# Eight more groups of unread products, and a new hand-written order, in a gated delta-rule layer with a softplus MLP

## The chip, the cores and the metric

The kernel runs on one core of one Trainium2 chip. A core has five engines that work side by side, each through a queue of its own: TensorE (PE, matrix products; its weight loads are shown as PEld), VectorE (DVE), ScalarE (ACT), GpSimd (POOL) and SyncE (SP, which here only issues DMAs). The metric is the device time of one execution in microseconds (us); lower is better. A profile is one execution recorded by the hardware profiler.

## The reference, cut to what matters

There are 4 batches of 8 heads, 768 time steps, and 48 features a head. Each head keeps a 48x48 state and runs a gated delta rule; its output, in the layout of 3072 tokens by 384 features, goes through a two-layer network with softplus between.

```python
k_n = k / (np.linalg.norm(k, axis=-1, keepdims=True) + 1e-06)
for t in range(S):
    readout = np.einsum('bhd,bhde->bhe', q[:, :, t], state)
    y[:, :, t] = g[:, :, t] * readout
    v_old = np.einsum('bhde,bhd->bhe', state, kt)
    state = state + bt[:, :, :, None] * np.einsum('bhd,bhe->bhde', kt, vt - v_old)
...
h = x @ w_in                                             # 384 -> 2048
g = np.maximum(h, 0.0) + np.log1p(np.exp(-np.abs(h)))
return (g @ w_out).astype(np.float32)                    # 2048 -> 384
```

## The kernel before

The 768 steps are cut into 12 chunks of 64. Within a chunk the recurrence is rewritten as dense algebra: the Gram matrix of the keys, the inverse of a unit triangular 64x64 matrix for each of the 32 heads, and products with the state that came from the chunk before. Two chunks make a pair; what is said of "inverse 2" is the inverse of the pair of chunks 2 and 3.

The program is built as a list of numbered items. Each has a kind, the engines that may run it, the items that it depends on and the buffers that it uses. Nothing runs in the order in which items are added. A table, `_ORDER`, is read word by word by `emit` (lines 56 to 74). A word such as `D178` says that item 178 is issued now, on VectorE (P is TensorE, D VectorE, A ScalarE, G GpSimd, S SyncE). So the table fixes each engine's own order and, where an item may run on more than one engine, which one does it. It also fixes who gets which buffer: an item's buffer is taken from a ring at the item's first use and goes back after its last use, so an item can have to wait until the last reader of the buffer's former content is done. Which engine is ahead of which is not fixed: that comes out of semaphores on the chip.

The rings that matter: PSUM has five buffers `d` for all products of the scan, two `h` for the first dense layer, and one `o` for the second and for the unread products. Loaded queries (`qf`) have two buffers, loaded keys (`kf`) three, query tiles in half precision (`qn`) two.

The kinds of items, in the order of a pair's work, with their lines:

- `load` (lines 249 and 271): the inputs, by DMAs in SyncE's queue. `wload` (297): quarters of the two weight matrices, `w0` and `w1`, by DMAs in GpSimd's queue.
- `ksq`, `red` (545, 549): squares of the keys on ScalarE, and their sums on VectorE. The root follows: `sqrt` on ScalarE for the first two pairs, `pow` on GpSimd (566) for the others. `eps` (570, 572) adds the small constant and inverts.
- `cast`, `kmul` (327): keys and queries to half precision, the keys times their inverse norm (but for the first pair, which is scaled later). `trs` (345, 388): transposes on TensorE. `kev`: their copy out of PSUM into `kqt`.
- `gram` (503; `gramk`, `gramq`, `gramd` at 461 and 432 for the first pair): products of keys with keys and queries. `kkc` copies the key part to `kk`, `mask` (518, 480) the masked query part.
- `kd0`, `kd1`, `ln` (604, 611): the diagonal blocks are gathered and transposed into a layout in which each partition holds two 16x16 blocks. `clear`, `diag`, `prep` (629) and 15 `step`s (639, 646) then invert those blocks row by row: two small instructions to a step, each dependent on the one before, on VectorE for the first pair and on GpSimd for the other five.
- `cv`, `tn` (667) and `c16`, `t32` (686): two copies of the result, and their transposes. `xmm` (707), `xs`, `tmm` (732), `tlo`, `thi` and `zmm` (770), `z` (779): the blocks are put together to the larger inverse. `xmm` is the first product that reads the inverse.
- The scan of a chunk, for even and odd heads apart: `ks`, `qs` (813; state times keys and queries), `vs` (823; values of the first pair times the norm), `w` (847), `umm` (855), `u1`, `zu` (878), `u2`, `smm` (898) and `s` (913; the new state), `ymm` (928), `y` (943; the output times the gate `g`), `ytr` (962) and `xt` (transposed for the dense part).
- The dense part of a chunk or pair: `g1` (992) in groups of six products, `soft` (1004; softplus on ScalarE), `g2` (1019) in groups of four, `o` (copy) and `store` (1039). Between the roots and the first softplus ScalarE loads another table of functions (`table`, line 1051).
- `warm` (1064): groups of three products of the identity with itself, 512 columns wide, into an `o` buffer. Nothing reads them. `IDLE` (line 98) is the number of groups: 24, in the table as P1232 to P1255. Four groups share one buffer.

Before, the 24 groups stand as follows in TensorE's queue: 15 of them (1232 to 1243, 1248 to 1250) among the transposes and Gram products of the first pair, up to the transposes of q2; two (1251, 1244) right behind the last Gram product of chunk 0; three (1245 to 1247) between the transposes of q3 and `xmm` of chunk 0; and the other four (1255, 1254, 1252, 1253) among the first groups of `g1` and the scan of chunk 1.

Of the kernel before, what the change touches and what calls it, by code (L numbers as in the profile page):

```python
# [74 lines left out]
def kernel(  # L75
# [19 lines left out]
    DM = H * D  # L95
    RAW = (0,)
    ON_ACT = (0, 1)
    IDLE = 24
    FF = moe_w_in.shape[1]
    NF = FF // P  # L100

# [954 lines left out]
    for cs in jobs:  # L1056
        dense(cs)
    for x in range(IDLE // 4):
        wb = Buf(p_o)
# [12 lines left out]


_ORDER = """
S0 D158 P1232 P1234 P1233 P1235 A1 P1236 P1238 D111 P1237 P1239 P114 A9 A104 D105 A110 P112 S8
A106 D115 P1241 D113 P124 P121 A123 D134 P137 A138 D133 P135 P1243 D125 P147 D107 D122 A136 P144
A108 P1240 P127 P1242 A149 P1249 A148 A146 D126 P1248 D109 D156 S19 S18 A145 S2 P1250 A206 P207
S3 A116 A117 A208 P118 A120 S5 S17 A119 P150 A152 S12 A129 S33 A154 D159 S27 S26 D157 D160 D161
D162 D163 D164 D165 D166 D167 D168 D169 D170 D171 P128 S16 D172 D173 D174 P1251 D175 D176 D177
P1244 A197 S25 D198 A222 P223 A224 G179 S11 A140 D178 G238 G239 P1245 A131 P1246 P1247 S24 A199  # L1080
P181 D180 S10 A139 P184 A182 D200 S4 D588 D132 D130 G188 A185 G187 P183 A190 P193 D194 A189 A594
P595 S13 A589 S32 P590 A201 D202 D203 D219 P186 A596 A591 P597 A598 P592 P605 A593 P603 S7 S6
D606 D604 A191 P204 P609 P607 A587 S34 D192 A275 D205 P209 D608 P214 S35 S42 S43 D211 A610 D210
D216 P220 G96 A212 A217 A215 D213 P141 A221 A142 A143 D218 D276 S41 S40 A277 P600 P599 D601 D602
P195 G300 D196 P872 D278 G99 A873 P230 A231 P225 A228 P1255 A226 A233 A235 D232 D229 D227 D611
D234 P874 A875 P886 D236 P619 P612 D620 D613 P151 D155 A284 P884 G98 A887 A885 G97 S14 D237 P285
P1254 A286 P882 P301 A883 A302 P615 A616 S49 P622 A623 P876 S15 A877 P878 G100 G101 G103 P614
P617 G279 D280 P621 P624 D153 S48 A879 A625 A618 G102 D281 P282 D297 P1252 D283 P630 D631 P632
D633 P292 A293 P298 A299 P880 A881 P634 A295 G240 G241 D294 D635 G242 G243 G244 G245 G246 P1253
G247 G248 P303 A304 G249 G250 G251 G252 G253 D306 D307 S50 P308 D296 A309 A311 P904 A905 P916  # L1090
A917 D312 P287 A290 D288 A313 P914 G254 G255 G256 D305 A915 P888 P910 A911 D314 D315 P627 P626
D629 D628 A353 D257 D258 P912 A913 P908 D354 P889 G259 D260 A909 G316 G317 P906 A907 G318 G319
G320 P902 A903 P890 P891 S57 A892 S56 P261 A262 G321 A267 P264 D265 A355 P895 P896 D291 P638
P266 P263 A270 D289 P643 P636 D310 G322 P897 P898 A268 P271 D356 G357 S20 S21 D644 A269 A899
P646 A647 D637 P639 A640 P918 S51 D362 P363 D272 A364 P641 A642 P645 P648 A649 S59 S58 A378 D358
P919 P920 P921 A922 D359 P650 P651 D653 P654 D652 S22 S23 D655 P656 P273 P925 P379 D657 A380
D274 P660 P667 P658 G323 G324 G325 G326 G327 A659 P926 P669 S28 S29 D668 G375 P670 A671 S65 S64
A431 D661 P663 D664 P927 D432 P672 A673 P662 P665 A666 S31 P360 D361 P376 S30 P678 D679 A377
P680 D681 P365 A366 D367 A368 D369 P928 P682 D683 P381 D383 A384 G328 G329 G330 G331 G332 G333
P386 A389 D388 D387 P956 S72 S73 A433 D385 A957 D434 P962 P370 D371 D390 D372 A963 A373 A382  # L1100
P954 A955 P936 A937 A391 P675 S74 P674 P934 G334 A935 G335 D336 S66 D374 S67 G440 G337 D676 S894
S36 D338 D677 D392 P944 S901 A945 S923 P342 A343 D393 P339 P952 A953 S37 S44 A340 A346 P948 A949
P441 P940 A941 A345 P684 P691 D692 D685 A442 P341 P693 P344 D348 G435 D436 A347 D453 P942 A943
S75 P932 A933 P349 P687 P694 S81 S80 P686 G394 S45 D350 A509 G395 G396 G397 G456 G398 P960 G399
S924 S39 A695 A961 A929 P950 D688 P689 D690 P454 S38 A951 P946 A947 P938 S88 A939 P457 G400 A458
G401 G402 G403 G404 G405 D510 P958 A959 S89 P964 G406 G407 S893 S931 S91 P702 D703 S930 S90 P351
S54 P696 D697 D352 A511 D512 P965 P966 P967 D968 S970 G408 G409 G410 P698 A455 P459 A462 D461
D463 P699 D460 D700 P971 P972 D701 P973 P974 P464 D437 S900 P704 A975 S85 S969 P708 A465 P438
D468 A467 D466 D709 D705 P978 P715 D716 P711 A439 A712 P979 P448 D450 D452 D451 D449 P718 S47
S46 S60 G534 G411 S53 G412 A415 A719 D416 P710 P713 A714 P980 P981 P443 D445 D447 P717 P720 A982  # L1110
S52 A444 P726 D727 P985 A721 P706 A446 A469 P728 A424 D729 P722 P723 P535 A536 P730 D707 P986
P987 D731 P1000 S55 G513 A1001 P1014 A1015 D470 S83 D471 A423 P988 A989 P1008 P1010 G413 A1009
D414 P420 A1011 P417 A418 D724 D514 D725 D531 P1018 A1019 P994 A995 A421 P532 D533 D515 P998
A999 P739 P732 D733 S82 A518 P734 P419 P422 D740 G472 G473 G474 G475 D426 P1004 A1005 D425 P996
A997 P429 P427 P742 D430 A743 P735 A736 P1002 D428 A1003 P519 P741 P744 P737 G476 A745 P1020
A1021 D738 S991 S70 D520 G477 S983 P516 P1006 P750 D751 S977 A517 A1007 S69 S976 P542 D544 D545
A543 D546 P752 P992 S71 A993 D753 P1016 A1017 P521 D523 A522 D525 P746 A524 P747 S990 D748 D749
P1022 A1023 P1012 G478 G479 G480 A1013 G481 P526 D530 A527 A529 P537 A540 D539 D538 P763 D541
P1024 P1025 P754 S984 P1026 P1027 D528 P756 P758 S84 A755 S61 D764 P766 S87 A1028 G482 G483 G484
G485 G486 G487 G488 G489 G490 G491 D492 P495 S63 P498 S62 D757 S1030 A767 A499 A496 G547 P759  # L1120
D548 D549 P1031 P1032 P1033 P1034 A1035 S1037 P765 D760 G493 D494 A501 A502 P768 D769 P761 D762
P1038 P1039 P776 D777 P771 P774 P497 P500 S76 A503 P770 D775 P778 D779 P1040 P1041 A1042 P1070
A1071 P1062 A1063 P1045 P1072 A1073 S68 S1036 P1058 A1059 P1046 P1054 A1055 P1074 D772 D773 P780
D781 P787 P1047 A1075 P1048 A1049 P1064 A1065 S77 S1043 P1060 A1061 P783 A784 D788 P790 A791
G550 G551 G552 G553 G554 G555 G556 G557 G558 G559 G560 G561 G562 G563 G564 D504 P505 P1056 S78
A1057 P1080 A1081 P782 D506 P785 D786 G565 G566 G567 G568 G569 G571 P789 P792 D793 P1052 A1053
P1066 A1067 P798 D799 P794 P795 D796 P1078 A1079 D797 P1082 P804 D805 A1083 P813 P811 D812 S79
P507 P807 D572 D508 A580 D570 S1050 S1044 S93 D808 P800 D801 S1029 P814 D815 P1068 A1069 P1076
A1077 P1084 P1085 P1086 P1087 D1088 P816 A817 P806 P809 D810 S95 P576 P573 A574 S1051 P824 D825
P802 A803 S1089 P1091 P1092 P1093 P1094 P818 P822 D823 A577 P578 A1095 S1097 P575 A581 P819 D582  # L1130
D820 P826 A827 S1090 P1098 P1099 P1100 P1101 A1102 S86 S94 S1103 P1132 A1133 P1114 A1115 P1105
P1126 A1127 D821 P828 P837 D829 P835 P583 P1138 A1139 P1116 A1117 P1106 P1107 P1120 A1121 P1108
A1109 S1111 S92 P1140 A1141 D836 D584 D579 P838 A839 P831 A832 P1134 A1135 P1128 A1129 P840 A841
P830 P833 P1112 A1113 S1104 S1110 P848 D834 P846 P843 P842 P1118 A1119 P1130 A1131 D844 D845
P852 P859 P1122 D847 A1123 D849 P850 D851 D860 D853 P1124 A1125 P1142 A1143 P1144 P1136 P1145
P1146 A1137 P1184 A1185 P1147 D1148 S1149 S1150 P1178 P862 D863 P855 D856 P585 D586 A1179 P1158
P1159 P1160 P1161 A1162 P854 P857 A858 P861 P864 P1151 P1152 P1153 P1154 D1155 S1156 S1157 P1172
D865 P1174 P1165 P1166 A1173 A1175 P1167 P1168 D1169 S1170 S1096 P1182 A1183 P1176 A1177 P868
D869 P866 D867 P1186 A1187 P1180 A1181 P870 S1171 P1188 P1189 D871 P1204 A1205 P1208 A1209 P1190
P1191 A1192 S1194 P1206 A1207 S1193 P1212 A1213 P1195 P1196 P1202 P1210 A1203 A1211 P1197 P1198  # L1140
D1199 S1200 S1201 P1216 A1217 P1214 S1163 P1218 P1219 P1220 A1215 P1221 A1222 S1223 S1164 S1224
P1225 P1226 P1227 P1228 A1229 S1231 S1230
"""

# [1 line left out]
_INS = ['q', 'k', 'v', 'beta', 'g', 'moe_w_in', 'moe_w_out']  # L1146
_OUTS = [((3072, 384), 'float32')]


# [23 lines left out]
```

## Time and profile before

| | |
|---|---|
| Median of the runs (lowest, highest) | 255.66 us (254.85, 256.0) |
| The profiled execution's own time | 255.46 us |
| Its span, from the first to the last instruction | 253.6 us |
| PE busy | 236.9 us (93%) |
| DVE, ACT, POOL busy | 153.7, 153.0, 127.1 us |
| Mean granted TensorE clock | 0.966 |
| DMA | 27.56 MB, 109 GB/s in the mean |
| The unread products (line 1064) | 72, 19.3 us busy |
| First dense layer (992), second (1019) | 73.3 and 70.3 us busy, 384 products each |

Busy time counts each engine for itself. The granted clock is the share of its full speed that TensorE was allowed: here 1.00 or 0.50. Matrix products overlap in the array, so that a product's duration is longer than the distance to the next one; what a group costs in a full queue is read from start to start. In a row of the timeline, "x32" counts instructions and the bracket at the end gives the engine's pause before them and what ended it.

### The profile page before, as it was taken

The page shows a single profiled execution, that of the slowest core. Times are in us where ns is not written, and L with a number is a line of the kernel's source. Part 1 is how long each engine was busy: PE and PEld are TensorE (multiplying, and loading weights), DVE is VectorE, ACT ScalarE, POOL GpSimd, SP SyncE. Part 2 cuts the span into 40 slices and gives each one's busy share as a digit, 9 for nine tenths or more (in the row PEclk, how much of TensorE's full clock was granted, in tenths as well). Part 3 has the DMA queues.
Part 4 walks back from the last instruction along what each step waited for, and adds up shares of the span by engine and source line. Part 5 has one row for each costly group of instructions (what it writes and reads, how often), then busy time and mean ns, then how long its engine had stood idle before and what let it go on. Part 6 is the DMA issues. An engine that isn't in the chain of part 4 may idle for free.

```text
span 253.6 us, 11355 instructions
## 1 busy us (share of the span) xinstructions
PE 236.9 (93%) x5040; PEld 160.5 (63%) x5040; DVE 153.7 (61%) x311; ACT 153.0 (60%) x285; POOL 127.1 (50%) x227
## 2 busy tenths in 40 slices
PE   7976588998989999999999999999999999999993
PEld 3543577676766765666766767755676565777751
DVE  7789888775893699759697588523843315313000
ACT  3557777686866579973777675456453475223530
POOL 8201653978879889988948859884000000000000
PEclk9999757799999999999999999999999999999999
DMA  8999999999990789083943850643024130112113
GB/s 111 198 181 178 178 179 180 186 195 176 176 153 6 173 180 157 4 200 83 156 98 84 170 99 22 124 83 80 3 66 93 23 80 0 34 32 48 34 47 78
DMA packets 86192, 27.56 MB, mean 109 GB/s; under 512 B 76288, under 2 KB 86144, under 8 KB 86144
## 3 DMA queue, kind: packets, MB, share of 16 engines
q1 hardware_dynamic: 80096, 23.21, 50.2%
q0 software_dynamic: 3968, 3.25, 8.2%
q10 hardware_dynamic: 2080, 0.39, 1.2%
q8 instruction: 39, 0.64, 1.2%
q14 instruction: 9, 0.07, 0.1%
HBM read 25.26 MB, written 4.72 MB: 118 GB/s over the span
## 4 chain that ended last, share of the span: by engine, by line
PE 76%; DVE 9%; DMA 4%; issue 3%; SPq 2%; ACT 2%; POOL 2%; ACTq 0%; DVEq 0%; POOLq 0%
PE h L992 25%; PE o L1019 23%; PE d L813 4%; DMA beta_l<-in_beta_dram 3%; PE d L855 3%; PE d L732 3%; PE d L770 3%; PE d L878 2%; PE d L928 2%; PE d L503 2%; PE d L707 2%; PE d L898 2%; PE d L388 2%; PE d L345 2%; POOL beta_l L175 2%
## 5 line engine op out<-in xcount | busy, mean ns | idle before, releaser
L1004 ACT ACTIVATE ga<-h 128x512 f16<-128x512 f32 x96 | 56.3, 598 | 33.4 <-PE h L992 27.6
L992 PE MATMUL h<-xt,w_in 128*128 128x512 f16 (+1 forms) x384 | 73.3, 330 | 0.1
L1019 PE MATMUL o<-w_out,ga 128*128 128x384 f16 x384 | 70.3, 326 | 1.4 <-issue 0.7
L1019 PEld LDWEIGHTS <-ga 128*128 128x128 f16 x384 | 35.7, 98 | 23.9 <-issue 1.8
L992 PEld LDWEIGHTS <-w_in 128*128 128x128 f16 x384 | 35.6, 99 | 20.7 <-issue 0.6
L639 POOL TENSOR_TENSOR tmp<-nn,tt 128x30 f32<-128x30 f32 (+7 forms) x75 | 30.1, 401 | 5.6
L646 POOL TENSOR_TENSOR tt<-tt,tmp 128x30 f32<-128x30 f32 (+7 forms) x75 | 29.4, 392 | 5.9
L566 POOL TENSOR_TENSOR nv<-nv,half_c 128x32 f32<-128x32 f32 x4 | 21.8, 5456 | 5.1 <-DVE nv L549 5.1
L218 ACT ACTIVATE kqt<-d 128x1024 f16<-128x1024 f16 (+1 forms) x21 | 18.4, 903 | 7.0 <-PE d L388 6.1
L218 ACT ACTIVATE osb<-o 128x384 f32<-128x384 f32 x18 | 8.8, 489 | 21.5 <-PE o L1019 21.4
L943 DVE TENSOR_TENSOR yg<-d,gf 128x384 f16<-128x384 f32 x24 | 12.8, 553 | 13.6 <-PE d L928 10.2
L1064 PE MATMUL o<-ident 128*128 128x512 f16 x72 | 19.3, 411 | 1.4 <-POOL ident masks.py:199 1.4
L847 DVE TENSOR_TENSOR w<-vf,d 128x384 f16<-128x384 f32 x22 | 11.3, 549 | 12.0 <-PE d L813 10.8
L218 ACT ACTIVATE u<-d 128x384 f16<-128x384 f32 x31 | 14.3, 491 | 7.1 <-PE d L878 3.3
L218 ACT ACTIVATE kk<-d 128x256 f16<-128x256 f32 (+1 forms) x34 | 12.8, 413 | 7.8 <-PE d L503 6.4
L518 DVE TENSOR_TENSOR mt<-d,mask 128x256 f16<-128x256 f32 x40 | 15.5, 418 | 3.2 <-PE d L503 1.9
L220 DVE CAST u<-d 128x384 f16<-128x384 f32 x17 | 9.1, 549 | 13.1 <-PE d L878 11.6
L813 PEld LDWEIGHTS <-kqt 48*64 48x64 f16 x704 | 13.3, 108 | 5.5 <-issue 5.3
L220 DVE COPY osb<-o 128x384 f32<-128x384 f32 x6 | 3.3, 556 | 21.6 <-PE o L1019 21.6
L813 PE MATMUL d<-s,kqt 48*64 48x48 f16 x704 | 16.4, 188 | 0.0
L545 ACT ACTIVATE ksq<-kf 128x768 f32<-128x768 f32 x12 | 10.1, 843 | 7.6 <-DMA kf<-in_k_dram 6.7
L220 POOL CAST tw<-tt 128x256 f16<-128x256 f32 x10 | 5.4, 563 | 16.1 <-DVE tt L646 16.0
(110 smaller groups left out, 380.1 us busy)
## 6 DMA issues: line engine op xcount, KB each, us to landing
qf<-in_q_dram SPq DMA_DIRECT2D x24, 192.0 KB, 5.1
vf<-in_v_dram SPq DMA_DIRECT2D x24, 192.0 KB, 5.2
gf<-in_g_dram SPq DMA_DIRECT2D x24, 192.0 KB, 4.2
out_dram<-osb SPq DMA_DIRECT2D x48, 96.0 KB, 2.4
kf<-in_k_dram SPq DMA_DIRECT2D x22, 192.0 KB, 5.1
w_in<-in_moe_w_in_dram POOLq DMA_DIRECT2D x4, 384.0 KB, 7.5
w_out<-in_moe_w_out_dram POOLq DMA_DIRECT2D x4, 384.0 KB, 12.9
kf<-in_k_dram ACTq DMA_DIRECT2D x2, 192.0 KB, 7.5
```

Source lines behind the costliest of these rows:

```text
L218: nc.scalar.activation(o, x, AF.Copy, scale=float(sign))
L220: ENG[en].tensor_copy(o, x)
L518: nc.vector.tensor_tensor(mt[c][m].ap[:, NP * p : NP * p + NP], gb[m].ap.rearrange("p (n b) -> p n b", n=NP)[:, :, C:], mask[:, None, :].b ...
L566: lambda en: nc.gpsimd.tensor_tensor(nv.ap, nv.ap, half_c, ALU.pow),
L639: eng.tensor_tensor(t, nn.ap[:, :, j + 1 :, j : j + 1].broadcast_to([P, 2, n, w]), tt.ap[:, :, j : j + 1, :w].broadcast_to([P, 2, n, w]), ...
L646: eng.tensor_tensor(rows, rows, t, ALU.add)
L813: nc.tensor.matmul(hd(o.ap)[HALF[r], NP * p + i], kq_of(c)[FEAT[m], 8 * p + 2 * i + r, off : off + C], s0[r].ap[FEAT[m], NP * p + i], **st ...
L943: lambda en, m=m: nc.vector.tensor_tensor(heads(yg.ap, m), hd(yp[m].ap), heads(gf.ap, m), ALU.mult),
L992: nc.tensor.matmul(hp.ap[:, n * b : n * b + n], w_in[:, j, f * P : (f + 1) * P], xt.ap[:, j, t0 : t0 + n], start=(j == 0), stop=(j == 2),)
L1004: lambda en, hp=hp, o=gb: nc.scalar.activation(o.ap, hp.ap, AF.Softplus),
L1019: nc.tensor.matmul(op.ap[:, :DM], b.ap[:, col + c0 : col + c0 + 128], w_out[:, f, :], start=(f == 0), stop=(f == NF - 1),)
L1064: nc.tensor.matmul(wb.ap.rearrange("p (a b) -> p a b", a=4), ident, ident[:, None, :].broadcast_to([P, 4, P]),)
```

## The change

`IDLE` goes from 24 to 32, which adds eight groups of three unread products, P1256 to P1263. And `_ORDER` is a new table. It has the same 1232 working items and the same dependences. Of the first 87 words of the new table, 83 are among the first 87 of the old one, and each engine's own order is as before over that part: at least the first 30 items of TensorE, 33 of VectorE, 20 of ScalarE and 18 of SyncE's queue are the same; behind it the order of all five queues is new. 90 items have changed engines: VectorE has 13 items more, ScalarE 15 fewer, GpSimd 2 more.

The diff, cut to its core: the table up to the first reader of the inverse of chunks 2 and 3 (`P261`, `P264`), line for line from the first new group on.

```diff
-    IDLE = 24
+    IDLE = 32
...
-D162 D163 D164 D165 D166 D167 D168 D169 D170 D171 P128 S16 D172 D173 D174 P1251 D175 D176 D177
-P1244 A197 S25 D198 A222 P223 A224 G179 S11 A140 D178 G238 G239 P1245 A131 P1246 P1247 S24 A199
-P181 D180 S10 A139 P184 A182 D200 S4 D588 D132 D130 G188 A185 G187 P183 A190 P193 D194 A189 A594
-P595 S13 A589 S32 P590 A201 D202 D203 D219 P186 A596 A591 P597 A598 P592 P605 A593 P603 S7 S6
-D606 D604 A191 P204 P609 P607 A587 S34 D192 A275 D205 P209 D608 P214 S35 S42 S43 D211 A610 D210
-D216 P220 G96 A212 A217 A215 D213 P141 A221 A142 A143 D218 D276 S41 S40 A277 P600 P599 D601 D602
-P195 G300 D196 P872 D278 G99 A873 P230 A231 P225 A228 P1255 A226 A233 A235 D232 D229 D227 D611
-D234 P874 A875 P886 D236 P619 P612 D620 D613 P151 D155 A284 P884 G98 A887 A885 G97 S14 D237 P285
-P1254 A286 P882 P301 A883 A302 P615 A616 S49 P622 A623 P876 S15 A877 P878 G100 G101 G103 P614
-P617 G279 D280 P621 P624 D153 S48 A879 A625 A618 G102 D281 P282 D297 P1252 D283 P630 D631 P632
-D633 P292 A293 P298 A299 P880 A881 P634 A295 G240 G241 D294 D635 G242 G243 G244 G245 G246 P1253
...
-P626 D629 D628 A353 D257 D258 P912 A913 P908 D354 P889 G259 D260 A909 G316 G317 P906 A907 G318 G319
-G320 P902 A903 P890 P891 S57 A892 S56 P261 A262 G321 A267 P264 D265 A355 P895 P896 D291 P638
...
+D173 P1244 P1247 D174 D175 D176 D177 D178 P1245 P1246 A154 P181 D130 S4 P1258 A140 D198 A179
+D180 S7 A139 S43 P1257 A222 P184 A182 P183 D588 D132 P1256 A199 D190 S32 P1259 S13 S6 G188 P193
+D200 D194 S35 S42 S34 A589 A189 G238 P223 G187 P590 A201 D202 D219 D203 A594 A591 G96 S41 S23
+P595 A596 P1262 G284 S40 P597 A598 A185 P592 D593 P605 D606 A224 P186 D191 P603 D604 P204 D205
+P607 A192 P609 D610 A608 A275 S66 P214 G239 A217 P1263 A215 A587 P209 A212 G99 D611 S14 D216
+D218 D276 S15 D213 P599 P600 D602 D601 A210 P872 A873 A277 G98 P220 A221 D211 P195 G100 G97 P141
+A143 G101 G300 P874 D196 D278 P225 D227 D226 A142 A228 P230 D232 D231 S50 D234 S67 S51 D233 P884
+A875 P886 D229 P619 A885 A887 D620 A235 G279 P285 A286 P614 D236 D237 S65 D280 P882 P301 G103
+P621 D297 A302 P1260 P612 P622 G102 P880 D613 S48 P1261 A881 G240 P151 P1253 S49 D623 P624 A625
+D153 G241 D155 G242 P876 G243 G244 G245 G246 G247 G248 D281 P615 D616 P632 P1254 G249 G250 S56
+G251 S57 P282 D283 S21 S64 A877 A883 P617 D633 P298 A618 P1252 P292 D293 A299 P630 A295 P287
+D631 P634 A290 A288 D291 D289 P1255 A635 G252 G253 G254 G255 G256 G257 D296 D440 P303 D306 D307
+D294 D304 D305 P308 A311 A309 P878 P888 A879 A313 D312 D314 D315 P916 A917 P889 P902 A903 A259
+D260 P627 D310 P890 P891 P912 P904 A913 A892 S894 D258 G316 G317 G318 G319 P626 D629 G320 G321
+G322 G268 G323 D628 P908 A909 S75 A905 A355 D356 P264 P261 D262 P895 P896 A265 P910 A353 P266
...
```

To read it: P1256 to P1263 are the new groups; P223 is `trs` of q3, P181 and P184 `xmm` of chunks 0 and 1, P183 and P186 their `tmm`, P193 and P195 `zmm`, P872 the first `g1`, P225 and P230 `gram` of chunk 3; P906, P910 and P914 are `g1` 1.4, 1.8 and 1.12. D178 and D180 are `tn` and `t32` of the first pair, D198 `red` 2, D278 `red` 5, D236 and D237 `kd1` and `ln` of the second pair, D258 its `tn`; G188, G187 and G238 are the `tlo` halves of the first pair and the `clear` of the second, G240 and G241 `prep`, G242 to G256 the steps, G257 and D257 `cv` of the second pair, A259 and G259 its `c16`; A587 is `table`, A221 the copy of k3 out of PSUM, A235 `kd0`, G279 `pow`; S43 is a half of q5, S66 a half of q8.

## The prediction

> **What bounds the kernel now.** I read the page's slices first, then the busy time by stage, then the timeline of each engine around the places where TensorE (PE) stops. The slices:
>
> ```profile
> PE   7976588998989999999999999999999999999993
> POOL 8201653978879889988948859884000000000000
> PEclk9999757799999999999999999999999999999999
> ```
>
> A slice is 6.34 us. PE is full from the eighth slice on; it loses time in slices 3 to 7, where the granted clock falls as well. The same by stage (columns: stretch, length, then busy time and count for PE, PEld, DVE, ACT, POOL, then clock, DMA share, GB/s):
>
> ```profile
> 19.70:28.00 8.30, 4.85 (x84) 2.65 (x76) 7.75 (x22) 5.41 (x10) 1.67 (x4) 1.00 1.04 164
> 28.00:41.70 13.70, 11.88 (x327) 10.79 (x323) 10.82 (x22) 10.91 (x24) 9.27 (x10) 0.50 1.08 185
> 41.70:45.10 3.40, 2.06 (x64) 1.52 (x61) 2.83 (x5) 1.85 (x5) 0.81 (x1) 1.00 1.22 191
> 45.10:48.50 3.40, 3.40 (x14) 1.91 (x13) 2.99 (x5) 2.85 (x6) 3.40 (x1) 0.50 1.26 185
> 48.50:70.50 22.00, 21.12 (x432) 16.20 (x430) 16.14 (x29) 16.57 (x31) 17.93 (x39) 1.00 1.05 181
> 70.50:249.40 178.90, 177.34 (x3852) 118.93 (x3851) 97.27 (x174) 104.82 (x193) 86.82 (x156) 1.00 0.43 84
> ```
>
> From 70.5 us PE is busy for 177.34 of 178.90 us: whatever stands behind a point in its queue there is paid in full. So the end is read at one cut, the `xmm` pair of chunks 2 and 3 (line 707). What sets that cut is the chain of waits (start, length, what):
>
> ```profile
> 60.09 0.65 PE o L1064 x3
> ...
> 64.85 1.45 DVE kkd L604
> ...
> 66.40 1.05 DVE ln L611
> 67.45 0.90 DVE s L913 x2
> 68.35 1.06 DVE tv L228 x2
> ...
> 69.44 1.06 DVE tn L667
> ...
> 70.54 1.19 PE d L707 x64
> ```
>
> PE reaches the pair at 70.34 and waits 0.20 us for the transposed inverse `tn`: PE and the inverse arrive together. The inverse is POOL's work, from 51.86 us (`prep`) to 68.28 us (the last of 15 steps), and POOL's timeline holds the square root before it and a slow instruction in it:
>
> ```profile
> 44.29 5.46 POOL L566 TENSOR_TENSOR nv<-nv,half_c 128x32 f32<-128x32 f32 x1 [4.02 <-DVE nv L549]
> 65.29 1.19 POOL L639 TENSOR_TENSOR tmp<-nn,tt 128x78 f32<-128x78 f32 x1
> ```
>
> **The change part by part.** Counted in the two order tables, PE has the same items ahead of that cut, but for two differences: all eight new groups stand ahead of it, and three dense groups (`g1` 1.4, 1.8, 1.12) have moved behind it. A dense group takes 0.65 us start to start (twelve products, "61.31 1.43" in the chain, are two of them with a hand-over), so 1.96 us more is behind the cut. Hence, with equal losses behind it: change of the end = (time of the pair after − 70.54) + 1.96. Break-even is 68.6 us.
>
> 1. *Eight groups.* 0.65 us each in the row above, 5.2 us together; at half clock the chain has one at 1.35 us. Less the three dense groups, PE's queue up to the cut is 3.2 us longer: without any recovery it arrives at 70.34 + 3.2 = 73.6.
>
> 2. *Clock.* If it stays at 1.00, half of 11.88 and of 3.40 us comes back, 7.6 us at most; if it falls just the same, nothing. The new groups stand between `xmm` and `tmm` of chunk 1 and on to its `gram` (six of them), and two among chunk 1's scan.
>
> 3. *The holes.* Before, PE waited 1.61 us for q3's transposes and 1.83 us for `tn` of chunks 0/1. Now q3 stands behind `zmm` 0; five old groups run in one piece from 19.72 (3.24 us), to 22.96. On DVE the reduction `red` 2 (0.94) no longer stands between `cv` and `tn`, so `tn` ends at 26.3, not 27.15. One hole of 3.3 us is left in place of two. Gain in the sum: nothing, since the groups only fill PE's wait.
>
> 4. *From `tn` to the Gram products of chunk 2.* DVE now runs a mask (0.66) and `red` 2 (0.94) ahead of the transpose `t32`, which ends at 28.65 (28.01 before). POOL clears its tile (0.52) between the two halves `tlo` (1.57 and 1.55), so the second ends at 32.4 (31.2 before), and `umm` starts there instead of at 31.4. The products then run at full clock, and chunk 2's `gram` comes out at 37.85, against 37.87 before. The faster products pay for the later halves: nothing gained. If the clock falls there all the same, it is some 1 us later (`tmm`, a key transpose and `ytr` at double their time), which is in the own range below.
>
> 5. *From there to POOL's inverse.* ACT's softplus table (load 1.28, dummy 0.20) was in a pause before; it now stands in front of two copies of chunk 2. With `ksq` 5 (0.84) behind it too, the copy of chunk 3's keys (1.02) runs at 42.9 to 43.9 instead of 39.95 to 40.97. Chunk 3's `gram` starts at 43.9; DVE's seven reads of it (0.42 each) bring the last copy to 46.6 (46.0 before). `kd0` (1.15) is behind three softplus and ends at 48.55, `kd1` (1.28) at 49.9, `ln` (1.05) directly behind it at 50.9 (51.77 before, since two `w` and a mask stood between). POOL: root from 43.9, 5.46, then two weight loads of 0.8 each, free at 50.9. So `prep` starts at 50.9, a gain of 0.9.
>
> 6. *The inverse.* 16.4 us from `prep` to the last step, as before: the key multiplications (line 327) and `kd1` beside which POOL's slow instructions stand still fall into it. Bounds: 14.5 without the three slow instructions (0.84, 0.86, 1.19 against 0.25 to 0.34 of their kind), 17.4 with one more. I take the middle, the row itself: 67.3.
>
> 7. *Behind it.* `cv` moves from DVE (1.06) to POOL (1.86); the copy `c16` moves to ACT (0.93). On DVE, `t32` (1.03) and a mask (0.42) now come before `tn` (1.03): 0.93 + 1.03 + 0.42 + 1.03 = 3.4, against 70.50 − 68.28 = 2.2. `tn` ends at 70.7, and the pair starts at 70.8.
>
> 8. *Loads.* In SyncE's queue q5's second half now waits for its buffer until q1 is cast on ACT (about 26); k4, v1, g0, q4 stand behind it and go out between 26.6 and 30.2 instead of 21.5 to 28.3. By the landing medians (4.2 to 5.2) g0 is there before `y` at 35, and q4 at 35.3, where POOL's cast holds three weight loads for 0.5 us. The first weight quarter goes out at 33.2 (32.0 before) and lands at 40.7 by its median 7.5; at its slowest (10.1) `g1` slips by 2.6, beside the inverse, which hides it. Bounds on the end: 0 to +1.
>
> 9. *Later inverses.* POOL's tables gain a `c16`, halves and two key multiplications and lose `kd0` 10 (2.84) and the last `cv` and `c16`. The last `xmm` pair moves forward by 6 to 11 us of PE work, but POOL ended 13 us before it (173.8 against 186.4). Hidden; if the cover is gone, up to +2.
>
> Sum: PE would arrive at 73.6 − R. By points 3 to 5 R is 5.6, so it arrives at 68.0 and waits 2.8 for the pair. The pair is at 70.8: (70.8 − 70.54) + 1.96 = +2.2 us. Against the profiled execution's own time of 255.46 us (span 253.6, 0.20 under the median of 255.66) that is 257.7 us.
>
> The Trainium skill, page "TensorE: Matmul & The Clock Gate", part 1, says that the clock halves after an idle window of about 3.4 us and comes back after a busy one. The trace has only the two speeds, but halved at 28.0 with no PE pause over 1.83 us since 19.7, so the measurement says that thinly filled stretches count too. By that rule the new hole alone is about enough to halve it near 26, which is the third rival.
>
> **The rivals.**
>
> *Faster: the clock is the whole story.* R = 7.6 and the inverse is not the gate: 5.2 − 7.6 = −2.4, 253.1 us. It decides if the pair can start before 67.3 (0.5% of the time, 1.3 us, which is about what a measurement can tell from no change). For it: 15.3 us of PE work at half speed. Against: POOL's root would have to start by 40.3 instead of 43.9, and `red` 5 before it hangs on ACT and DVE, 80% busy there.
>
> *About the same: PE's arrival decides.* If POOL meets no slow instruction (14.5 us), `tn` is there at 68.8, PE at 68.0: (68.9 − 70.54) + 1.96 = +0.3, 255.8 us. Against: three such instructions in before.
>
> *Much slower: the change doesn't hold the clock.* If the hole at 23 to 26.3 us halves it, the four groups ahead of `zmm` 0 take 1.35 each (+2.8) and `tmm` and `zmm` about 1.0 instead of 0.5 each; less some slack on POOL and DVE the chain to the inverse is 3.5 us later, the pair at 74.3: +5.7, 261.2 us. For it: 0.78 us of unread products in the 3.4 us before 28.0 did not suffice. Against: in the 3.4 us from 24.6 two groups would now run.
>
> **How the numbers follow.** Forecast (pair held by the inverse) 0.39, own range 256.8 to 259.5, the top with half clock for one window after the 2.8 us pause (+1.7); same 0.21; faster 0.23; much slower 0.17. The range takes in the unknown terms and reaches to both outer rivals: 252.6 to 261.0. Faster by over 0.5%: 0.23; within: 0.22; slower: 0.55.
>
> **What would show it.** Step 2: clock 1.00 over 28 to 41.7. Step 3: PE's largest pause just before the first line-707 pair, which starts near 26.3. Step 5: root at 43.9, `prep` at 50.9. Steps 6, 7: second line-707 pair at 70.8 with PE waiting for `tn` of line 667. Behind it 178.9 + 2.0 us to PE's end. The prediction is wrong if that pair starts before 68.6, or if PE loses clearly more or less behind it than before.

## The result and the profile after

The changed kernel takes 265.82 us in the median (264.23 to 267.49, four runs), the kernel before, run beside it, 255.25 us (254.47 to 256.0, four runs). The ratio is 1.0394 (95% interval 1.0344 to 1.0444): slower by 3.9%. The forecast was 257.7 us, and the time lies outside its range of 252.6 to 261.0. The profiled execution took 265.06 us (span 263.3), 9.60 us more than that of before.

Ratios here and below leave out executions more than 1.5% above the fastest of the same kernel, so that a median over all of them can lie further from the kernel before than its ratio does.

The slices of the changed kernel (6.58 us each):

```profile
PE   7988889199989999999999999999999999999993
POOL 8200681198889988988898881882200000000000
PEclk9997986689999999999999999999999999999999
```

PE has a nearly empty slice, the eighth (46.1 to 52.7 us), that was not there before. The busy time by stage (columns as before: stretch, length, busy time and count of PE, PEld, DVE, ACT, POOL, clock, DMA share, GB/s):

```profile
24.10:37.60 13.50, 10.92 (x293) 7.21 (x291) 12.31 (x22) 8.38 (x18) 7.80 (x8) 1.00 0.95 158
37.70:44.40 6.70, 6.49 (x99) 4.41 (x101) 5.27 (x11) 4.59 (x10) 2.22 (x3) 0.50 1.30 177
44.60:47.80 3.20, 1.54 (x36) 1.19 (x30) 0.75 (x1) 0.00 (x0) 0.82 (x1) 1.00 1.25 187
48.00:54.70 6.70, 3.11 (x42) 2.33 (x43) 3.36 (x8) 4.09 (x7) 3.00 (x1) 0.50 1.22 223
54.80:79.50 24.70, 22.13 (x419) 15.46 (x418) 18.36 (x32) 15.10 (x26) 21.54 (x40) 1.00 0.70 102
79.50:259.00 179.50, 178.76 (x3870) 120.22 (x3869) 98.72 (x181) 99.46 (x183) 86.51 (x157) 1.00 0.45 85
```

From 44.6 to 54.7 us every engine has gaps, while the DMA share is over 1.2. The chain of waits says what they wait for (start, length, what):

```profile
34.48 0.61 SPq L249
35.14 1.01 SPq L249
36.20 13.49 DMA kf<-in_k_dram
...
51.59 1.07 PE d L503 x32
...
58.14 1.05 DVE ln L611
...
59.27 1.92 POOL nn L629 x2
...
78.49 0.94 DVE tn L667
79.48 1.19 PE d L707 x64
```

A load of keys, the second half of k5 (`S40` in the table; its first half is `S41`), was issued at 36.20 and landed 13.49 us later. The waits (us in all, times, longest) and ACT's and POOL's timelines show who stood behind it:

```profile
ACT ksq L545 <- DMA kf<-in_k_dram: 5.8, 1, 5.8
...
PE d L503 <- ACT kqt L218: 5.5, 1, 5.5
...
POOL nv L566 <- DVE nv L549: 5.3, 1, 5.3
```

```profile
49.79 0.84 ACT L545 ACTIVATE ksq<-kf 128x768 f32<-128x768 f32 x1 [5.84 <-DMA kf<-in_k_dram]
...
51.70 5.47 POOL L566 TENSOR_TENSOR nv<-nv,half_c 128x32 f32<-128x32 f32 x1 [5.32 <-DVE nv L549]
```

In the kernel before, the same two halves were issued ahead of the row of weight loads, and the squares didn't wait (SyncE's queue, POOL, ACT):

```profile
33.92 1.33 SPq L249 DMA_DIRECT2D kf<-in_k_dram  x2
...
35.66 2.33 POOL L297 DMA_DIRECT2D w_in<-in_moe_w_in_dram  x3
...
41.81 0.86 ACT L545 ACTIVATE ksq<-kf 128x768 f32<-128x768 f32 x1
```

In the changed kernel that row begins at 36.07, between the first half of k5 and the second:

```profile
36.07 1.56 POOL L297 DMA_DIRECT2D w_in<-in_moe_w_in_dram  x2
```

The squares of k5 ran at 49.79 instead of 41.81, so POOL's root started at 51.70 instead of 44.29. The difference of the two executions adds up at the cut that the prediction used:

| step | before | after | later by |
|---|---|---|---|
| root (`pow` 4) starts | 44.29 | 51.70 | 7.41 |
| root to `prep` | 7.57 | 7.57 | 0.00 |
| `prep` to the end of the last step | 16.4 | 17.0 | 0.6 |
| last step to the pair (line 707) | 2.3 | 3.2 | 0.9 |
| the pair starts | 70.54 | 79.48 | 8.94 |
| from the pair to the end (own time) | 184.92 | 185.58 | 0.66 |

8.94 + 0.66 = 9.60 us. Three quarters of the loss are in the first row. A second path runs from the same squares to `prep`: the copy of chunk 3's keys on ACT, its Gram products on PE, and `ln` on VectorE. It ended last, but by little: POOL was through with the root and two weight loads at 58.69, and `prep` waited 0.58 us more for VectorE. So taking only one of the two paths away can't give much back.

### The profile page after: what moved, and what is told of

Its sections match the earlier page's. It is cut to its first block, busy times and chain, and to the rows that moved or that the text cites. A ratio compares the mean times of both kernels' runs of the same rounds, so it can differ in the third digit from the quotient of the medians.

```text
span 263.3 us, 11384 instructions
## 1 busy us (share of the span) xinstructions
PE 244.7 (93%) x5064; PEld 161.3 (61%) x5064; DVE 158.1 (60%) x325; ACT 144.9 (55%) x268; POOL 129.3 (49%) x227
## 3 DMA queue, kind: packets, MB, share of 16 engines
q10 hardware_dynamic: 2080, 0.39, 1.1%
## 4 chain that ended last, share of the span: by engine, by line
PE 75%; DVE 8%; POOL 6%; DMA 5%; ACT 2%; issue 2%; SPq 1%; ACTq 0%; POOLq 0%; DVEq 0%
PE o L1019 23%; PE h L992 22%; DMA kf<-in_k_dram 5%; PE o L1064 4%; PE d L813 4%; POOL tt L646 3%; PE d L707 3%; PE d L855 2%; PE d L878 2%; PE d L770 2%; PE d L928 2%; POOL tmp L639 2%; PE d L732 2%; PE d L503 2%; PE d L898 2%
## 5 line engine op out<-in xcount | busy, mean ns | idle before, releaser
L1004 ACT ACTIVATE ga<-h 128x512 f16<-128x512 f32 x96 | 56.1, 598 | 44.6 <-PE h L992 42.2
L992 PE MATMUL h<-xt,w_in 128*128 128x512 f16 (+1 forms) x384 | 74.5, 333 | 0.8 <-ACT ga L1004 0.8
L1019 PE MATMUL o<-w_out,ga 128*128 128x384 f16 x384 | 71.3, 327 | 0.6 <-ACT osb L218 0.6
L1019 PEld LDWEIGHTS <-ga 128*128 128x128 f16 x384 | 35.5, 98 | 22.9 <-issue 0.9
L639 POOL TENSOR_TENSOR tmp<-nn,tt 128x30 f32<-128x30 f32 (+7 forms) x75 | 27.8, 370 | 5.4
L1064 PE MATMUL o<-ident 128*128 128x512 f16 x96 | 28.5, 443 | 1.4 <-POOL ident masks.py:199 1.4
L218 ACT ACTIVATE kqt<-d 128x1024 f16<-128x1024 f16 (+1 forms) x20 | 17.3, 894 | 7.6 <-PE d L388 6.5
L847 DVE TENSOR_TENSOR w<-vf,d 128x384 f16<-128x384 f32 x22 | 11.6, 548 | 12.0 <-PE d L813 10.6
L220 DVE CAST u<-d 128x384 f16<-128x384 f32 x19 | 10.3, 551 | 12.3 <-PE d L855 7.2
L1064 PEld LDWEIGHTS <-ident 128*128 128x128 f16 x96 | 9.5, 110 | 12.9 <-issue 6.2
L228 POOL TENSOR_SCALAR to<-td,own 128x512 f16<-128x512 f16 x3 | 5.3, 1751 | 24.8 <-DVE td L686 24.8
L220 DVE COPY osb<-o 128x384 f32<-128x384 f32 x10 | 5.5, 554 | 17.4 <-PE o L1019 17.4
L218 ACT ACTIVATE osb<-o 128x384 f32<-128x384 f32 x14 | 6.8, 489 | 14.8 <-PE o L1019 14.8
```

What stands on the lines that cost most here:

```text
L218: nc.scalar.activation(o, x, AF.Copy, scale=float(sign))
L220: ENG[en].tensor_copy(o, x)
L639: eng.tensor_tensor(t, nn.ap[:, :, j + 1 :, j : j + 1].broadcast_to([P, 2, n, w]), tt.ap[:, :, j : j + 1, :w].broadcast_to([P, 2, n, w]), ...
L992: nc.tensor.matmul(hp.ap[:, n * b : n * b + n], w_in[:, j, f * P : (f + 1) * P], xt.ap[:, j, t0 : t0 + n], start=(j == 0), stop=(j == 2),)
L1004: lambda en, hp=hp, o=gb: nc.scalar.activation(o.ap, hp.ap, AF.Softplus),
L1019: nc.tensor.matmul(op.ap[:, :DM], b.ap[:, col + c0 : col + c0 + 128], w_out[:, f, :], start=(f == 0), stop=(f == NF - 1),)
```

## Experiments: why the load was late

Theory L: the second half of k5 was issued just behind the first of the five weight loads that GpSimd issues one after the other (36.07 to 39.9 us), and beside these SyncE's queue is slow; before, it was issued at 34.6 to 35.25, ahead of the first of that row of weight loads (35.66). Rivals: the clock, which fell elsewhere (three stretches at half speed); the groups themselves, in front of PE's Gram products; and the wait of ACT's and PE's queues behind the squares of k5, whatever POOL's root does.

**The key load first.** In the changed kernel the second half of k5 goes ahead of a half of g2:

```diff
-... A594 A591 G96 S41 S23 P595 A596 P1262 G284 S40 P597 ...
+... A594 A591 G96 S41 S40 S23 P595 A596 P1262 G284 P597 ...
```

> The changed kernel with one load moved: the second half of k5 goes out before the half of g2, so ahead of POOL's weight loads. Theory L (k5 stands behind the weight loads in the DMA engines, and the squares of k5 hold up both ScalarE's queue and the root): from issue to landing 6 us or less instead of 13.5, squares of k5 at about 44 instead of 49.8, chunk 3's Gram products at 46 instead of 51.6, the root on POOL at 46 instead of 51.7, the second line-707 pair at 73.7 instead of 79.5, the end 5.7 us earlier: 259.4 us (258 to 261). Theory C (the half-clock stretches with the new groups in them are the cost): the stretch from 37.7 us stays, and so does the time, 264 to 266 us.

Measured: ratio to before 1.0116 (1.008 to 1.0153), median 258.89 us, profiled execution 257.62. Its timeline (SyncE's queue, ACT, POOL, PE):

```profile
34.79 1.33 SPq L249 DMA_DIRECT2D kf<-in_k_dram  x2
...
42.64 0.86 ACT L545 ACTIVATE ksq<-kf 128x768 f32<-128x768 f32 x1
...
45.32 5.47 POOL L566 TENSOR_TENSOR nv<-nv,half_c 128x32 f32<-128x32 f32 x1 [0.69 <-DVE nv L549]
...
52.32 1.32 POOL L629 TENSOR_TENSOR nn<-ln,beta_l 128x256 f32<-128x256 f16 x2
...
71.87 1.19 PE L707 MATMUL d<-tn,kk 64*64 64x32 f16 x64 [0.99 <-DVE tn L667]
```

Both halves are issued by 36.12, and nothing waits for them any more. One word moved forward in SyncE's queue gives back 7.4 of the 9.6 us (265.06 − 257.62). What is left, +2.16 us, is the sum that the prediction made without this load: (71.87 − 70.54) + 1.96, less 1.1 us by which the part behind the pair is shorter than that sum took it.

**Weight loads first.** The same kernel, but with the five weight loads moved ahead of the query cast, so that they are issued from 33.66 on instead of 36.07, around the key load that now precedes g2:

```diff
-... P595 A596 P1262 G284 S40 P597 ...
+... S40 S23 P595 A596 P1262 G99 G98 G100 G97 G101 G284 P597 ...
```

> The kernel with k5 first (258.9 us), and POOL's five weight loads issued ahead of its cast of q4 instead of behind it, so at 33 to 37 us, ahead of or beside k5's (34.8 and 35.5); SyncE's queue is unchanged, the half of g2 still behind k5. If the weight loads hold k5 back: it lands at 46 us or later again, the squares of k5 at 46 to 50, the root at 48 to 52, about 262 to 266 us. If the half of g2 ahead of it was what held it back: squares at 42.6 to 44, root at 45, 257 to 260 us.

Measured: 268.34 us (two runs), ratio 1.0476 (1.0412 to 1.0539). From its chain of waits:

```profile
35.00 17.61 DMA kf<-in_k_dram
```

Issued at 35.00, earlier than in the version above (35.45) and ahead of g2, the load takes 17.61 us. So it is not g2 in SyncE's own queue that holds it back, but the weight loads in GpSimd's.

**The kernel before, with the load late.** In the table of before, a half of g2 is taken ahead of the second half of k5 (its former place, further back, is not shown):

```diff
-... D218 D276 S41 S40 A277 ...
+... D218 D276 S41 S23 S40 A277 ...
```

> The kernel before with that one feature of the change: the half of g2 goes out between the two halves of k5, so that the second goes out at about 36.3, behind the first of POOL's weight loads (35.7), instead of at 34.6. If this place is the whole of the excess: k5 lands at 46 us or later, the squares at 46 to 50 instead of 41.8, the root at 48 to 52 instead of 44.3, the second line-707 pair 4 to 8 us later, 259 to 264 us. If the change's time comes from the other moves: within 1.5 us of before, 254 to 257 us.

Measured: two runs that differ, 256.75 and 263.22 us; there is no ratio. The profile is of the slower one, and its chain reads like that of the changed kernel:

```profile
34.51 1.80 SPq L249
36.30 0.04 issue
36.35 15.36 DMA kf<-in_k_dram
```

So the same wait for the load can arise in the old table too, without a new group; one run shows it. The other run's 256.75 us would fit a load that was early enough; it was not profiled, and that stays an inference.

**What the two queues move.** The DMA view of the changed kernel for 43 to 47 us, while the load waits:

```profile
q0 software_dynamic: 740, 0.60, 93.2%
q1 hardware_dynamic: 725, 0.14, 31.1%
```

and that of the kernel before for 36 to 38 us, while k5 passes:

```profile
q1 hardware_dynamic: 1640, 0.31, 92.5%
q0 software_dynamic: 32, 0.03, 14.2%
```

(Columns: packets, MB, share of the 16 engines; q0 is GpSimd's queue with the weights, q1 SyncE's.) Nearly alone, SyncE's queue moves 820 packets in a us, 155 KB. Beside the weight loads both queues get about as many packets, 185 and 181 in a us; but a weight packet is 811 bytes in the mean and a key packet 193, so that the weights move at 150 KB and the keys at 35 KB in a us. The Trainium skill, page "DMA: Bandwidth & Descriptors", section "Queues, rings and completion order", says that a DMA engine takes turns between the queues that have work for it, a whole packet at a time. The counts here, 740 against 725, agree with that, if what the profile counts as a packet is one in the page's sense; no run here shows whether it is.

The turns are not the whole of the 13.49 us. A half of k5 is 1024 packets of 192 bytes; at 181 in a us these need 5.7 us (an estimate). Ahead of them, from 36 to 40 us, SyncE's queue moved 2080 packets, about the two loads that were issued before (2 × 1024). And from 40 to 42 us it moved one packet, while GpSimd's queue went on:

```profile
q0 software_dynamic: 347, 0.34, 114.7%
q1 hardware_dynamic: 1, 0.00, 0.1%
```

So nearly 6 of the 13.49 us had passed before the load's own packets ran, some 2 of them with SyncE's queue standing still. What held it still there is open.

**Two of the five weight loads later.** In the changed kernel two of them go behind the root:

```diff
-... P195 G100 G97 P141 A143 G101 G300 ... P882 P301 G103 ...
+... P195 G97 P141 A143 G300 ... P882 P301 G100 G101 G103 ...
```

> The changed kernel with the first two quarters of the second weight matrix loaded behind the root of inverse 4 instead of ahead of it; SyncE's queue as it is. Theory L: two of the five weight loads ahead of k5 are gone, 384 KB each at the 145 GB/s that their queue moves, so k5 lands 5.3 us earlier, at 44.4; POOL has two issues more (1.6 us) between root and inverse, so the pair comes 3.7 us earlier: 261.4 us (259.5 to 263). If the half of g2 ahead of it, not the weights, is what delays k5: landing as before at 49.7, the end 1.6 us later than in the changed kernel, 267 us. Theory C: 264 to 267 us.

Measured: ratio 1.0407 (1.0319 to 1.0495). A miss: the squares of k5 ran at 48.62, only 1.2 us earlier. Three weight loads are left beside the load of k5, which was now issued at 36.48, and GpSimd's queue is through with them at about 47; from 47 to 49 SyncE's queue moves 1484 packets and GpSimd's 110. So the load came through, as it seems, only when the weights were nearly done, and with two of them away that was only a little earlier. That the other queue's turns went to the three that were left would explain it, but no run shows it apart.

**The squares of k5 behind other work.** In the changed kernel they, their sum and the root go behind the gathering of chunk 2's blocks:

```diff
-... P872 A873 A277 G98 ... D196 D278 P225 ... D620 A235 G279 P285 ... D236 D237 S65 ...
+... P872 A873 G98 ... D196 P225 ... D620 A235 A277 P285 ... D236 D237 D278 G279 S65 ...
```

> The changed kernel with the squares of k5 behind kd0 on ScalarE and their sum behind ln on VectorE, so that chunk 3's key copy and Gram products no longer queue behind the late load; the load itself is as late. If the path from the load goes by POOL's root (its result is wanted by POOL's own queue before the inverse): Gram products at about 46, root still at about 51.7, the pair at 79 and the end within 1 us of the changed kernel's: 264 to 267 us. If the path goes by ScalarE's queue and PE's pause before the Gram products: the pair at about 74, 259 to 261 us. Theory C: 264 to 267 us.

Measured: ratio 1.0317 (1.0211 to 1.0423). ACT is no longer held, and PE gets chunk 3's Gram products at once; the squares still wait:

```profile
43.57 0.64 PE L503 MATMUL d<-kqt 48*64 48x128 f16 x32
...
49.62 0.84 ACT L545 ACTIVATE ksq<-kf 128x768 f32<-128x768 f32 x1 [2.14 <-DMA kf<-in_k_dram]
...
51.53 5.47 POOL L566 TENSOR_TENSOR nv<-nv,half_c 128x32 f32<-128x32 f32 x1 [7.65 <-DVE nv L549]
```

PE's 5.45 us pause is gone and the profiled end is only 1.5 us earlier (263.55 against 265.06). `prep` starts at 58.53, 0.74 us earlier than in the changed kernel, and now follows POOL's own work. The path that is left is the root on POOL: the inverse of chunks 2 and 3 stands behind it in POOL's queue, though it doesn't need its result.

**Without the groups.** The new table with the eight words P1256 to P1263 left out and `IDLE = 24`; it leaves out only the unread products:

```diff
-    IDLE = 32
+    IDLE = 24
...
-D173 P1244 P1247 D174 D175 D176 D177 D178 P1245 P1246 A154 P181 D130 S4 P1258 A140 ...
+D173 P1244 P1247 D174 D175 D176 D177 D178 P1245 P1246 A154 P181 D130 S4 A140 ...
```

> The changed kernel's order without the eight new groups (24 groups). Theory L: all eight stand ahead of the second line-707 pair, where PE waits anyway, so the end stays within 1.5 us of the changed kernel's: 264 to 267 us; the clock should fall to 0.50 somewhere between 24 and 37.7, where it was 1.00 with them. Theory C (eight groups are 5.2 us at full clock and up to 10 at half): 257 to 260 us.

Measured: 265.72 us, ratio 1.038 (1.0309 to 1.0451), the same as with them. Its stage of half speed is as long as in the kernel before:

```profile
31.30:45.00 13.70, 11.88 (x264) 10.15 (x265) 11.27 (x20) 8.59 (x18) 8.21 (x10) 0.50 1.03 171
```

So the eight groups do hold the clock, 24.1 to 37.6 at 1.00 with them, and in the changed kernel that is worth nothing: the squares of k5 run at 49.74 without and at 49.79 with them.

## Experiments: what the groups are worth once the load is early

**The groups in the old table.** Two behind `xmm` of chunk 0 (P181), two behind its `tmm`, one behind its `umm` (P590), one between the halves of chunk 2's Gram products (P209) and two behind the transposes of k3 (P220). The change has the last two later, among the scan of chunk 1:

```diff
-    IDLE = 24
+    IDLE = 32
...
-... A199 P181 D180 ... P183 A190 ... S32 P590 A201 ... P209 D608 ... P220 G96 ...
+... A199 P181 P1258 P1257 D180 ... P183 P1256 P1259 A190 ... S32 P590 P1262 A201 ... P209 P1263 D608 ... P220 P1260 P1261 G96 ...
```

> The kernel before with the eight new groups alone, in the places that they have in the change (two behind the first xmm, two behind the first tmm, one each behind umm and gram of chunk 2, two behind k3's transposes), the rest of the order unchanged. By the clock theory: 1.00 from 28 to 41.7, PE's arrival at the pair at 68 to 70, the inverse up to 1.5 us earlier, 253.5 to 255.5 us (ratio 0.99 to 1.00). If the groups are worth no more than they cost: ratio 0.998 to 1.01. If the clock falls nonetheless: 5 us slower.

Measured: ratio 1.0181 (1.0062 to 1.0299). The clock is 1.00 from 22.9 to 50.2, and yet it is slower: the key multiplication that frees the buffer of k5 comes later, its second half is issued at 35.40 to 37.00 against 35.35 for the weight load, and the squares run at 48.82. None of the three cases written down names this.

**The same, with `ln` early.** In addition `ln` of chunk 2's pair directly behind the first decayed key, and the last weight load ahead of the root:

```diff
-... P612 D620 D613 ... G97 S14 D237 P285 ... P614 P617 G279 ... A618 G102 D281 ...
+... P612 D237 D620 D613 ... G97 S14 P285 ... P614 P617 G102 G279 ... A618 D281 ...
```

> The same, with the transpose ln of the second pair directly behind kd1 on VectorE (before, two w and a mask stood between) and the last weight load ahead of POOL's root instead of behind it. Between the root's end and prep POOL then waits for neither: prep at about 50 instead of 51.9 and the pair at about 68.5 to 69.5 if PE is there by then. 252.5 to 255 us, ratio 0.985 to 0.998. If PE's arrival decides: as the kernel with the groups alone.

Measured: ratio 1.013 (1.0064 to 1.0195). The squares ran at 52.86 and the root at 54.77 in the profile (263.68 us, the slowest of four runs), so that what `ln` gives can't be seen in it. Inconclusive on `ln`; the load is late again.

**A guard.** In the old table the clearing of POOL's tile and its diagonal (0.8 us) go directly ahead of the first of the row of weight loads:

```diff
-... A140 D178 G238 G239 P1245 ... D196 P872 D278 G99 A873 ...
+... A140 D178 P1245 ... D196 P872 D278 G238 G239 G99 A873 ...
```

> The kernel before with the clearing of tile 2 and its diagonal copy on POOL (0.8 us together) moved from ahead of the tlo cast to directly ahead of the first of the five weight loads, so that k5's second half is issued some 1.2 us ahead of the weight loads instead of 0.4. Theory (the second half of k5 races the weight loads): in this kernel k5 lands by 41.8 as in the kernel before and nothing waits for it; ratio 0.993 to 1.003. Rival (the margin is of no account, the loads of the changed kernel were late by their own place): the same ratio, but then the version with the groups and this guard is as slow as the one without the guard. If the two moved operations are wanted earlier than I think, the pair of chunks 2 and 3 begins over 1 us later than 70.5 and the ratio is over 1.004.

Measured: ratio 1.0002 (0.9968 to 1.0036). No change, as the theory has it where the load was in time anyway. In its profile (257.42 us) the squares of k5 run at 42.32, but the pair starts at 72.26, 1.7 us later than in the profile before, by PE's own queue; the ratio over all runs shows no such loss. The smaller spread that one might hope for isn't there (253.71 to 260.43).

**Guard and `ln`.** Both edits, without new groups:

```diff
-... A140 D178 G238 G239 P1245 ... D196 P872 D278 G99 A873 ... P612 D620 D613 ... G97 S14 D237 P285 ... P614 P617 G279 ... A618 G102 D281 ...
+... A140 D178 P1245 ... D196 P872 D278 G238 G239 G99 A873 ... P612 D237 D620 D613 ... G97 S14 P285 ... P614 P617 G102 G279 ... A618 D281 ...
```

> The same guard, and the logarithm of the roots of chunk 2 (ln 2 on DVE) directly behind the first decayed key, with the last weight load on POOL moved ahead of the root (pow 4). Expected: the inverse's preparation starts at about 50 instead of 51.9, the pair of chunks 2 and 3 then waits for TensorE's own queue (70.3) and not for the inverse; at most 0.3 us are to be had, ratio 0.990 to 1.002. If the weight load in front of the root delays it by more than the logarithm gains, the preparation starts after 52 and the ratio is over 1.002.

Measured: ratio 0.998 (0.9934 to 1.0025), no difference that can be told. In the profile (256.77 us, an execution outside the ratio) `prep` starts at 50.17 instead of 51.86; PE reached the pair later than that, at 71.60, by its own queue.

**Guard and eight groups.** The groups where the first version of this part has them:

```diff
-... A140 D178 G238 G239 P1245 ... A199 P181 D180 ... P183 A190 ... S32 P590 A201 ... P209 D608 ... P220 G96 ... D196 P872 D278 G99 A873 ...
+... A140 D178 P1245 ... A199 P181 P1258 P1257 D180 ... P183 P1256 P1259 A190 ... S32 P590 P1262 A201 ... P209 P1263 D608 ... P220 P1260 P1261 G96 ... D196 P872 D278 G238 G239 G99 A873 ...
```

> The kernel before with the eight groups of unread products and the guard. Theory (the groups cost by delaying k5's issue into the weight loads): the squares of k5 run at 42 to 43 instead of 48.8, the pair of chunks 2 and 3 begins at 70.5 to 72, the clock is 1.00 through 24 to 40, ratio 0.995 to 1.008. Rival (the groups themselves hold TensorE up, whatever k5 does): the pair begins at 73 or later with the squares of k5 at 42 to 43, ratio over 1.012. If the guard of 0.8 us is too short, the squares of k5 still run at 47 or later, and the pair at 75.

Measured: ratio 1.0055 (1.0000 to 1.0110), against 1.0181 without the guard. From its timeline:

```profile
44.95 0.85 ACT L545 ACTIVATE ksq<-kf 128x768 f32<-128x768 f32 x1
...
72.22 1.19 PE L707 MATMUL d<-tn,kk 64*64 64x32 f16 x64 [1.00 <-DVE tn L667]
```

No wait for the load any more. The squares are still 3 us late, because ACT takes them behind copies of Gram products, and these stand behind three new groups in PE's queue (one at 39.38 at half speed, 1.4 us, and two at 42.04, 1.3 us). So both the theory and its rival seem to hold a part here: by the profiles the pair starts 3.6 us earlier than without the guard (75.82), and still 1.7 us later than in the kernel before. By the times this isn't settled: the two intervals overlap, and five of the ten executions took 259.9 to 264.6 us and stand outside the ratio. None of these five was profiled, so that the guard may have failed in some of them.

**Guard, `ln` and four groups, none ahead of chunk 2's Gram products.**

```diff
-    IDLE = 24
+    IDLE = 28
...
-... A140 D178 G238 G239 P1245 ... A199 P181 D180 ... P183 A190 ... S32 P590 A201 ... D278 G99 A873 ... P612 D620 ... S14 D237 P285 ... P617 G279 ... A618 G102 D281 ...
+... A140 D178 P1245 ... A199 P181 P1256 P1257 D180 ... P183 P1258 A190 ... S32 P590 P1259 A201 ... D278 G238 G239 G99 A873 ... P612 D237 D620 ... S14 P285 ... P617 G102 G279 ... A618 D281 ...
```

The groups stand behind `xmm` (two), `tmm` and `umm` of chunk 0; the text below, written before the run, misnames the places.

> The kernel before with four of the eight groups (two behind the first xmm of chunk 1, one behind the second, one behind tmm; none ahead of chunk 2's gram), the guard on POOL, and ln 2 directly behind the first decayed key with the last weight load ahead of the root. Four groups fill pauses that TensorE has there anyway. If the groups' clock is worth something once k5 is on time and the inverse starts at about 50: the pair of chunks 2 and 3 begins at 69 to 70.3 instead of 70.5, ratio 0.990 to 0.998. If the clock only falls a window later, as in the version with eight groups and the guard (half speed at about 38 to 42), the pair stays at 70.5 to 71.5 and the ratio is 0.998 to 1.005. If the squares of k5 run after 44, the second key load still meets the weight loads, and the ratio is over 1.005.

Measured: ratio 1.0009 (0.9968 to 1.0051). The middle case came true in the time, though not by the way it named: the clock didn't fall. In the profile (256.47 us) it is 1.00 from 24 to the end, the root starts at 43.43, `prep` at 48.89, 3 us before that of the kernel before. PE comes to the pair at 70.16, 0.4 us earlier. Where the 3 us went, by PE's timeline and the chain of waits:

```profile
55.56 0.53 PE L928 MATMUL d<-u,mt 64*64 64x48 f16 x23 [1.60 <-issue]
...
59.22 0.51 PE L962 MATMUL d<-ident,yg 128*128 128x128 f16 x6 [1.62 <-DVE yg L943]
...
70.16 1.19 PE L707 MATMUL d<-tn,kk 64*64 64x32 f16 x64
```

```profile
39.16 18.79 DMA gf<-in_g_dram
```

`tn` is ready at 69.5 and PE's queue is what is late: it waited for the gated output `yg`, and that for a load of g that was issued at 39.16, beside the weight loads, and landed 18.79 us later, at 57.95. In the kernel before the same product `yg` ran at 57.92, when its load had come. So full clock and an earlier inverse end at the next load behind the same weights. Five of its twelve executions took 259 to 269 us; these were not profiled, and whether the load of k5 lost its race there is open. No version that beats the kernel before was found.

## Why the prediction was wrong

The step that failed is step 8, the loads: "By the landing medians (4.2 to 5.2)", with "Bounds on the end: 0 to +1". It measured +7.4 us (265.06 − 257.62). It spoke of k4, g0, q4 and of the first weight quarter, and didn't name k5, which had moved behind a half of g2 and past the first weight load; and it priced loads by their median over the whole run, where loads beside the weights took 10.6 to 19.5 us in the DMA views of the kernel before and of the version with the key load first. The trace of before had this in its DMA view for 36 to 38 us (median us from issue to landing at the end of the row):

```profile
gf<-in_g_dram SPq DMA_DIRECT2D x1, 192.0 KB, 11.9
kf<-in_k_dram SPq DMA_DIRECT2D x1, 192.0 KB, 15.3
```

These two halves were issued at 35.30 and 37.08, right beside the weight loads, and nothing waited for them early. Read as the price of a load in that place, they would have given the bound: k5 issued at 36.2 lands at 48 to 51.5.

The other steps, by the changed kernel, and by the version with the key load first, in which the failed step is taken out:

| step | forecast | after | key load first |
|---|---|---|---|
| 3, `xmm` of chunk 0 | 26.3 | 26.48 | 25.63 |
| 4, chunk 2's `gram` | 37.85 | 38.66 | 38.66 |
| 5, root starts | 43.9 | 51.70 | 45.32 |
| 5, `prep` | 50.9 | 59.27 | 52.32 |
| 6, `prep` to the last step, us | 16.4 | 17.0 | 16.3 |
| 7, the pair | 70.8 | 79.48 | 71.87 |
| PE reaches the pair | 68.0, waits 2.8 | 78.50, waits 0.98 | 70.88, waits 0.99 |
| from the pair to the end, us | 186.9 | 185.6 | 185.75 |
| profiled execution, us | 257.7 | 265.06 | 257.62 |

- *Step 1* (three dense groups behind the cut, 1.96 us) and the equal losses behind it were 1.1 to 1.3 us too dear. In the changed kernel PE was busy behind the pair for 178.76 us against 177.34, so 1.42 us more and not 1.96, and it was idle there for 0.74 us against 1.56. The eight groups' own 5.2 us never came to the path.
- *Step 2, the clock.* Right that it stays at 1.00 over most of the stretch (24.1 to 37.6), wrong in that it holds: it fell at 37.7, and again at 48, some 1.9 us into PE's pause of 5.45 us. Neither set the end: without the groups the slow stretches lie elsewhere, and the squares of k5 and the time are the same.
- *Steps 3 and 4* came within 0.2 and 0.8 us in the changed kernel. *Step 5* was 1.4 us early even with the load in time; *steps 6 and 7* held within 0.1 and 0.3 us there. PE's arrival, worked out by steps 1 to 5 with a recovery R of 5.6 us, was 2.9 us too early: 70.88 against 68.0, so that R was 2.7. That stayed without effect, since the inverse came later still. That this version's 257.62 is so near to the 257.7 is partly luck: the pair came 1.07 us later than forecast, and the part behind it was 1.1 us shorter. By the ratio it is at 1.0116 of before, where the forecast had 1.009 (257.7 / 255.46).
- *Step 9* (later inverses hidden): PE was busy for 178.76 of 179.50 us behind the pair; right.

The rivals: *faster by the clock alone* fell, since the version with the key load first has half speed in one window of 3.4 us only of the 228 us behind 24 (25.8 to 29.2) and is still 1.2% slower. *About the same* needed 14.5 us from `prep` to the last step and got 16.3 with the key load first. *Much slower*, 261.2, named the wrong cause: the hole before `xmm` was there (PE waited 1.17 us) and the clock did not fall behind it; in the version with the key load first it did, behind a pause of 2.80 us, for one window, and that was cheap. No rival was a late load.

## What to carry to other kernels

A load's price is that of the place where it is issued, not its median: look in the DMA view for what was issued beside the same traffic, and put that into the range whenever a new order moves a small-packet load past a large one, in whichever queue. Where two engines' queues are ordered only by when they get there, here some 0.8 us decided over 7; a load that something needs soon belongs ahead of the bulk loads by a margin that has to be measured; to put the bulk loads behind something that it releases would not depend on a margin, but no run here tried it. And unread products that hold the clock were worth nothing here while the inverse or a load, not TensorE, came last.

## What the hardware showed unexpectedly

Beside GpSimd's weight loads SyncE's queue moved 35 KB in a us where it had moved 155: the two got about as many packets (181 and 185 a us), not as many bytes. And some 2 to 6 us after the first of the row of weight loads was issued, SyncE's queue stood still for a while: one packet from 40 to 42 us in the changed kernel, against 347 of GpSimd's; and in the version with the weight loads first none from 36 to 38 us, against 327, though both halves of k5 had been issued by 35.9. A load issued 0.1 us behind the first weight load took 13.49 us, in the version with the key load first it was issued 0.8 us ahead of it (35.45 against 36.23) and took 4.8 us by its row of the DMA view. But a lead is no sure guard: in the version with the guard alone a half of g was issued 0.8 us ahead of the first weight load (35.37 against 36.19) and took 13.7 us. And the granted clock does not go with how busy PE is in the same stretch: in the changed kernel it was 1.00 from 44.6 to 47.8, with PE busy for 1.54 of 3.20 us, and 0.50 from 37.7 to 44.4, with PE busy for 6.49 of 6.70.
